# Expert 0's token weights read later, and the head's casts and patterns split between engines: a sorted-attention and expert-mixture kernel

## The chip, the cores and the metric

One core of a Trainium2 chip. TensorE (PE) multiplies matrices; VectorE (DVE), ScalarE (ACT) and GpSimd (POOL) do elementwise work; SyncE (SP) issues DMA transfers, as POOL does too. The metric is the device time of one execution in microseconds (us). The time before is the median of three runs, 358.14 us (358.12 to 358.28).

## The reference

Two stages, with 4 batches, 8 heads, 768 tokens a batch, head size 64, 8 blocks of 96 tokens, 4 experts, model width 512 and hidden width 1024.

```
P = sort_net                                  # 4 x 8 x 8 x 8
for _ in range(5):
    P = exp(P - max); P = P / row sums; P = P / column sums
k_sorted = einsum('bhij,bhjcd->bhicd', P, k blocks)     # and v_sorted
attn = softmax(scale * q_block @ k_sorted_block^T)
x = (attn @ v_sorted), as 3072 tokens x 512
p = domain_probs / (domain_probs.sum(-1) + 1e-9)        # 3072 x 4
out = sum over e of p[:, e] * (relu(x @ w1[e]) @ w2[e])
```

## The kernel before

The order of every engine's instructions is the order of the program's text (`tc.manual_schedule()`); the framework adds the waits that the data and the buffers need. There are two parts. The head (up to about 37 us) works on batch 0's attention and on the first layers; after it, the attention of the later batches is threaded between the experts' products.

The head goes like this. `sort_net` is loaded as `sn` (32 rows of one head and batch each, L77). Five rounds of exponential (ACT, L310), row sums and column sums (DVE, L315 to L321) follow; the last column scaling is done together with a spreading over 16 columns into `sn16` (L330), rows 0 to 3 by DVE and rows 4 to 7 by POOL. `r_half(a)` (L340) turns four rows of it round with four matmuls into PSUM tile `ps_R`. `build_PI0` (L352) multiplies that with the mask `maskk` into the pattern `PI0`, four heads at a time. `mix_half` (L511) multiplies natural keys or values by the pattern, for 4 heads (`qd`), after some warm-up matmuls (`keep_warm`, L504); `mixed` (L529) casts the result from PSUM into `kT` or `vT0`, for blocks `i0` to `i0+n` of four. `h_w` transposes mixed values (L548) and copies them out (L553); `h_s` makes scores (L576) and their exponential (L582); `h_a` multiplies by the values (L593) and normalizes (L606, L607); `h_x` transposes into `xT` with the permutation `perm` (L624, L628); `group0` runs expert 0's first layer (L704), `second_layer0` its second (L741).

Loads of q, k, v and weights are issued by POOL, in text order, and POOL waits before an issue when the eighth load before it hasn't landed. SP issues `sort_net`, the token probabilities `p_in` (L170) and `p_own` (L171: for the first 768 tokens, 128 partitions x 6 x 4 values). From `p_in`, `spread_weights` makes the normalized weights `p_out`, in steps between the rounds; its last step (L252) is followed by SP's store of the first rows (L256), the broadcast load `pb` (L230), which waits for that store, and the store of the rest (L258). From `p_own`, `own_weights` (L261) makes `p_sb`, expert 0's weight of a token, with four DVE instructions; `second_layer0` scales by it (L748). In the text `own_weights` stands after the second `group0(0, 1, 1, ...)` (L1435). DVE's later order is: casts of `h_k` and `h_v` (L532), the query copy (L301, of `h_q_both`, the second half on ACT), the copy L553, the scaling L748.

POOL's constants, `perm` (L200), the zeroed tails of `kT` and `ET` (L206, L210) and the ones in `vs0` (L215), stand before its part of `sn16`.

Of the kernel before, what the change touches and what calls it, by code (L numbers as in the profile page):

```python
# [11 lines left out]
F16 = mybir.dt.float16  # L12
# [6 lines left out]
def kernel(  # L19
# [11 lines left out]
    nc = tc.nc  # L31

    B, H, S, D = q.shape
    GH = B * H
    NB = sort_net.shape[-1]
    BLK = S // NB
# [3 lines left out]
    P = 128  # L40
    SCALE = float(D) ** -0.5

    CP = P // NB
    R = BLK // CP
# [3 lines left out]
    HB = NB // 2  # L48
    VW = D + 2
# [6 lines left out]
    const = ctx.enter_context(tc.tile_pool(name="const", bufs=1))  # L56
# [19 lines left out]
    sn = const.tile([GH, NB, NB], F32, name="sn")  # L76
# [10 lines left out]
    def from_spare(n):  # L87
        at = spare["at"]
        spare["at"] += n
        return Sflat[:, ds(at, n)]  # L90
# [37 lines left out]
    def head(b, nm, h):  # L128
        return natural[(b, nm, h // 4)][:, h % 4, :, :]
# [20 lines left out]
    def load_half_queries(hf):  # L150
        for qd in range(2):
            nc.gpsimd.dma_start(
                q0[ds(64 * qd, 64), hf].rearrange("p h r d -> p h (r d)"), half_queries(qd, hf)
            )
# [7 lines left out]
    def p_part(at, n):  # L162
        return Tt[2].rearrange("p a f x -> p (a f x)")[:, ds(2 * at, 2 * n)].bitcast(F32)
# [4 lines left out]
    p_own = p_part(2 * E * NT + NT, R * E).rearrange("p (t e) -> p t e", e=E)  # L168
    own_den = p_part(2 * E * NT + NT + R * E, R).rearrange("p (t o) -> p t o", o=1)
    nc.sync.dma_start(p_in, moe_domain_probs.rearrange("(p t) e -> p t e", t=NT))  # L170
    nc.sync.dma_start(p_own, moe_domain_probs[0:S].rearrange("(t p) e -> p t e", p=P))  # L171
    load_half_queries(0)
    load_natural(0, "k", 0)

# [1 line left out]
    ident = const.tile([P, P], F16, name="ident")  # L176
# [4 lines left out]
    for kc in range(0, NKC, 2):  # L181
# [15 lines left out]
    )  # L197

    perm = const.tile([BLK, BLK], F16, name="perm")
    nc.gpsimd.tensor_copy(  # L200
        perm.rearrange("p (c r) -> p c r", r=R), ident[0:BLK, 0:BLK].rearrange("p (r c) -> p c r", c=CP)
    )
    kTs, ETs, vs0s, wide = [], [], [], []
    for n in range(2):
        kT = const.tile([P, S + 32], F16, name=f"kT_{n}")
        nc.gpsimd.memset(kT[:, ds(S, 32)], 0.0)  # L206
        kTs.append(kT)
    for n in range(4):
        ET = const.tile([P, S + 32], F16, name=f"ET_{n}")
        nc.gpsimd.memset(ET[0:BLK, ds(S, 32)], 0.0)  # L210
        ETs.append(ET[0:BLK])
        wide.append(ET)
    for n in range(2):
        vs0 = from_spare(HB * 4 * VW)[0:BLK].rearrange("c (i s h w) -> c i s h w", i=HB, s=2, h=2)
        nc.gpsimd.memset(vs0[:, :, :, :, ds(D, 2)], 1.0)  # L215
        vs0s.append(vs0)
    vo = arena[:, ds(4 * NW + NQ + 4 * 4 * P, R * 4 * VW)].rearrange("p (r h w) -> p r h w", r=R, h=4)


# [6 lines left out]
    def load_p(b, c, es=range(E), pb=None):  # L226
        if pb is None:
            pb = moe.tile([P, E, 2 * P], F32, name=f"pb_{b}_{c}", tag="pb", bufs=1)
        n = len(es)
        nc.sync.dma_start(  # L230
            pb[:, ds(es[0], n)],
            p_dram[ds(es[0], n), ds(b * S + 2 * c * P, 2 * P)].rearrange("(o e) x -> o e x", o=1).broadcast_to(
                [P, n, 2 * P]
            ),
        )
        return pb
# [7 lines left out]
    def spread_weights():  # L244

        nc.vector.tensor_reduce(p_den, p_in, AX.X, ALU.add)
        yield
        nc.vector.tensor_scalar(out=p_den, in0=p_den, scalar1=1e-9, scalar2=None, op0=ALU.add)
        yield
        nc.vector.reciprocal(p_den, p_den)  # L250
        yield
        nc.vector.tensor_tensor(  # L252
            p_out.rearrange("p e t -> p t e"), p_in, p_den.broadcast_to([P, NT, E]), ALU.mult
        )
        p_rows = p_dram.rearrange("e (p t) -> p e t", t=NT)
        nc.sync.dma_start(p_rows[0:S_P], p_out[0:S_P])  # L256
        pbs[(0, 0)] = load_p(0, 0)
        nc.sync.dma_start(p_rows[S_P:P], p_out[S_P:P])  # L258
        yield

    def own_weights():  # L261

        nc.vector.tensor_reduce(own_den, p_own, AX.X, ALU.add)
        nc.vector.tensor_scalar(out=own_den, in0=own_den, scalar1=1e-9, scalar2=None, op0=ALU.add)
        nc.vector.reciprocal(own_den, own_den)
        nc.vector.tensor_tensor(p_sb[:], p_own[:, :, 0:1], own_den, ALU.mult)
# [38 lines left out]
    scol = const.tile([GH, NB, 1], F32, name="scol")  # L305
    sn16 = const.tile([GH, NB, NB, CP], F16, name="sn16")
# [19 lines left out]
            if it:  # L326
                next(p_steps)

    for a, eng in enumerate((nc.vector, nc.gpsimd)):
        eng.tensor_tensor(  # L330
            sn16[:, ds(a * HB, HB)],
            sn[:, ds(a * HB, HB)].rearrange("g i (j o) -> g i j o", o=1).broadcast_to([GH, HB, NB, CP]),
            scol[:].rearrange("g j (i o) -> g i j o", i=1).broadcast_to([GH, HB, NB, CP]),
            ALU.mult,
        )

    ps_R = psM.tile([P, 2, 512], F32, tag="ps", name="ps_R")
    Rv = ps_R[:, :, 0:HB * GH].rearrange("p a (i g) -> p a i g", g=GH)
# [11 lines left out]
    Rs = const.tile([P, GH, NB], F16, name="Rs")  # L350

    def build_PI0(eng, a, h0, hn, src):  # L352
        eng.tensor_tensor(
            PI0[a][:, ds(h0, hn)],
            maskk[:, 0:HB * CP].rearrange("p (o i c) -> p o i c", o=1, c=CP).broadcast_to([P, hn, HB, CP]),
            src.rearrange("p g (i o) -> p g i o", o=1).broadcast_to([P, hn, HB, CP]),
            ALU.mult,
        )
# [18 lines left out]
            )  # L377

    r_half(0)
    for h0 in range(0, H, 4):  # L380
        build_PI0(nc.vector, 0, h0, 4, Rv[:, 0, :, ds(h0, 4)].rearrange("p i g -> p g i"))
    vec, act = nc.vector.tensor_copy, nc.scalar.copy


# [126 lines left out]
    def mix_half(nm, qd, hf, pool, warm_up=0):  # L511

        ps = pool([P, 1024], F32, f"ps_m{nm}_{qd}_{hf}")
        keep_warm(ps[:, 0:P], warm_up)
        tails[(nm, qd, hf)] = ps[:, 2 * R * 64:1024].bitcast(F16).rearrange("p (n x) -> p n x", n=2)
        ps = ps[:, 0:2 * R * 64].rearrange("p (s r x) -> p s r x", s=2, r=R)
        for sg in range(2):
            for r in range(R):
                for hh in range(2):
                    h = 4 * qd + 2 * sg + hh  # L520
                    nc.tensor.matmul(  # L521
                        ps[ds(D * hh, D), sg, r, :],
                        head(0, nm, h)[:, r, :],
                        PI0[hf][:, h, :, :].rearrange("p i c -> p (i c)"),
                        start=True, stop=True,
                    )
        return ps

    def mixed(nm, qd, ps, i0, n, copy):  # L529

        dst = kTs[qd][:, 0:S] if nm == "k" else vT0[qd]
        copy(  # L532
            dst.rearrange("p (i x c) -> p x i c", i=HB, c=CP)[:, :, ds(i0, n)],
            ps.rearrange("p s r (i c) -> p (s r) i c", c=CP)[:, :, ds(i0, n)],
        )
# [4 lines left out]
    def h_v(qd, hf, copy, pool=psa):  # L540
        mixed("v", qd, mix_half("v", qd, hf, pool), 0, HB, copy)
# [24 lines left out]
    def h_s(qd, qq, ps=None):  # L566

        kT, ET = kTs[qd], ETs[2 * qd + qq % 2]
        if ps is None:
            ps = psa([P, 2, 512], F32, f"ps_s0_{qd}_{qq}")  # L570
        for n in range(4):
            for hh in range(2):
                sg, i = n // 2, 2 * (qq % 2) + n % 2

                m = BLK if 2 * i + sg == 3 else P
                nc.tensor.matmul(  # L576
                    ps[0:m, hh, ds(n * BLK, BLK)],
                    kT[ds(D * hh, D), ds((2 * i + sg) * BLK, m)],
                    qT0[qd][ds(D * hh, D), sg, qq // 2, :, ds((2 * (qq % 2) + n % 2) * CP, CP)],
                    start=True, stop=True,  # L580
                )
        nc.scalar.activation(  # L582
            ET[:, 0:S].rearrange("c (h x) -> c h x", h=2), ps[0:BLK, :, 0:HS],
            AF.Exp, bias=0.0, scale=SCALE,
        )
# [426 lines left out]
    for e in range(E):  # L1012
        w, hk, hf = w1sb[e], NKC // 2, FF // 2
# [380 lines left out]
    ]  # L1394


    mk0 = mix_half("k", 0, 0, psm, 8)
    mixed("k", 0, mk0, 0, 2, act)
    mv0 = mix_half("v", 0, 0, psa)
    mixed("v", 0, mv0, 0, 2, vec)  # L1400
    r_half(1)
    act(Rs.rearrange("p g (a i) -> p a g i", a=2), Rv.rearrange("p a i g -> p a g i"))
    h_s(0, 0)
    mixed("k", 0, mk0, 2, 2, act)
    load_half_queries(1)
    load_w2(0, 2)
    build_PI0(nc.gpsimd, 1, 0, H, Rs[:, 0:H, HB:NB])
# [24 lines left out]
    even01()  # L1432
    w11(vec)
    group0(0, 1, 1, [0, 1])
    own_weights()  # L1435
    ps_s11 = ps_a10
    h_s(1, 1, ps_s11)
    evacuate00 = group0(0, 1, 0, [2, 3], True)
# [9 lines left out]
    group0(1, 1, 0, [2, 3])  # L1448
    h_v(0, 1, vec)
    h_v(1, 1, vec)  # L1450
    group0(1, 1, 1, [2, 3])


# [66 lines left out]
    for g in range(G0 + 1):  # L1520
        b, c = divmod(g, R // 2)
# [56 lines left out]
```

## Time and profile before

| | |
|---|---|
| median of 3 runs | 358.14 us |
| the profiled execution | 358.21 us |
| its span, first to last instruction | 356.3 us |
| PE busy | 350.4 us (98% of the span) |
| DVE, ACT, POOL busy | 277.5, 170.1, 137.6 us |
| DMA packets, software queue (POOL's issues) | 38720, 19.93 MB |
| DMA packets, hardware queue (SP's issues) | 35856, 19.67 MB |
| store L256: issue, length of the issue, issue to landing | 19.99 us, 0.35 us, 5.5 us |
| load L171: issue, issue to landing | 1.66 us, 3.9 us |

The span is what the profile covers; 1.9 us of the execution lie around it. A line of the profile names the engine, the source line, the operation, what is written and read, and, in square brackets, how long the engine sat idle before it and what ended that. PEld is TensorE's weight load, which overlaps its matmuls. Instructions are issued in order on each engine, so a wait holds up all that is behind it on that engine.

### The profile page before, as it was taken

The numbers are of one execution on the slowest core, as the hardware profiler recorded it, in microseconds if no ns is written. First come the engines' busy times: TensorE is split into PE (matmuls) and PEld (weight loads), VectorE is DVE, ScalarE is ACT, GpSimd is POOL, SyncE is SP. The second block draws the span as 40 slices with busy tenths as digits, with TensorE's granted clock in tenths as the row PEclk, the third lists the DMA queues.
The fourth block names the chain that finished last, engine by engine and source line by source line (L and its number), as shares of the span: only waits on it lengthen the run. The fifth ranks groups of instructions, "written<-read, shape, count | busy, mean of one in ns | idle before, by whom it ended". The sixth has DMA issues, their size and how long they took to land.

```text
span 356.3 us, 9511 instructions
## 1 busy us (share of the span) xinstructions
PE 350.4 (98%) x3948; PEld 305.5 (86%) x3948; DVE 277.5 (78%) x555; ACT 170.1 (48%) x302; POOL 137.6 (39%) x154
## 2 busy tenths in 40 slices
PE   8899999999999999999999999999999999999996
PEld 8686857888888888988899888888888888888886
DVE  5766787779798687778879988896678886588963
ACT  2653330452425445368847259830288611598301
POOL 8766112466022420000626318840068800188400
PEclk9999999999999999999999999999999999999999
DMA  8999999999999999743995410005200014100021
GB/s 104 203 205 230 212 209 194 207 195 167 195 180 166 195 116 203 138 88 44 180 205 91 107 74 0 2 1 136 78 26 3 2 37 141 62 0 2 0 75 46
DMA packets 74762, 40.26 MB, mean 113 GB/s; under 512 B 41568, under 2 KB 70496, under 8 KB 74720
## 3 DMA queue, kind: packets, MB, share of 16 engines
q0 software_dynamic: 38720, 19.93, 43.2%
q1 hardware_dynamic: 35856, 19.67, 27.2%
q8 instruction: 31, 0.51, 0.6%
q14 instruction: 11, 0.09, 0.1%
q10 hardware_dynamic: 144, 0.07, 0.1%
HBM read 41.88 MB, written 6.34 MB: 135 GB/s over the span
## 4 chain that ended last, share of the span: by engine, by line
PE 95%; DVE 3%; issue 0%; DMA 0%; ACT 0%; DVEq 0%
PE ps_h L815 18%; PE ps_Q L1296 18%; PE ps_p L799 12%; PE ps_X L1153 10%; PE ps_Z L1153 7%; PE ps_Q L1153 7%; PE ps_Z L1296 6%; PE ps_h L704 3%; PE ps_o L741 3%; PE ps_p L860 3%; PE ps_a L479 2%; PE ps_s L444 2%; PE ps_k L425 1%; PE ps_v L391 1%; PE ps_mv L521 1%; PE ps_a L593 0%
## 5 line engine op out<-in xcount | busy, mean ns | idle before, releaser
L815 PE MATMUL ps_h<-xT,w 128*128 128x256 f16 x576 | 67.5, 273 | 0.0
L815 PEld LDWEIGHTS <-w 128*128 128x128 f16 x576 | 55.2, 98 | 7.3
L821 DVE SCALAR_TENSOR_TENSOR Hb<-ps_h,pb 128x1024 f16<-128x1024 f32 x34 | 41.5, 1223 | 17.8 <-PE ps_h L815 17.6
L1153 PEld LDWEIGHTS <-w 128*128 128x128 f16 x480 | 43.6, 98 | 4.7
L1166 POOL TENSOR_TENSOR arena<-tmp,pb 128x512 f16<-128x512 f32 x12 | 15.2, 1276 | 65.7 <-PE ps_Z L1153 49.8
L1296 PEld LDWEIGHTS <-Hb 128*128 128x128 f16 x320 | 31.1, 98 | 3.5
L1165 ACT ACTIVATE tmp<-tmp 128x512 f32<-128x512 f32 x46 | 29.0, 632 | 3.9 <-DVE tmp L1203 3.9
L1296 PEld LDWEIGHTS <-Sb 128*128 128x128 f16 x304 | 28.2, 98 | 3.0
L1153 PEld LDWEIGHTS <-arena 128*128 128x128 f16 x312 | 27.7, 98 | 2.8
L451 ACT ACTIVATE ET<-ps_s 96x768 f16<-96x768 f32 x24 | 18.1, 802 | 25.2 <-PE ps_s L444 25.0
L434 ACT CAST kT<-ps_k 64x384 f16<-64x384 f32 x48 | 22.7, 473 | 13.3 <-PE ps_k L425 12.3
L126 POOL DMA_DIRECT2D arena<-in_q_dram x24 | 19.9, 842 | 20.8 <-DMA q_ring<-arena 17.7
L1153 PE MATMUL ps_X<-ET,arena 128*128 128x256 f16 x168 | 25.2, 272 | 0.0
L1296 PE MATMUL ps_Q<-w,Hb 128*128 128x256 f16 x192 | 24.6, 273 | 0.0
L799 PEld LDWEIGHTS <-Hb 128*128 128x128 f16 x232 | 21.9, 98 | 3.0
L1159 DVE SCALAR_TENSOR_TENSOR Hb<-ps_X,pb 128x512 f16<-128x512 f32 x27 | 18.7, 692 | 7.0 <-PE ps_X L1153 7.0
L1173 ACT COPY ps_X<-ps_Z 128x512 f32<-128x512 f32 x27 | 15.4, 571 | 17.8 <-PE ps_Z L1153 17.8
L1153 PE MATMUL ps_Z<-xT,w 128*128 128x256 f16 (+1 forms) x176 | 22.5, 258 | 0.0
L785 DVE TENSOR_TENSOR Sb<-Hb 128x512 f16<-128x512 f16 x33 | 20.6, 646 | 0.0
L1180 ACT COPY tmp<-ps_X 128x512 f32<-128x512 f32 x26 | 15.2, 586 | 9.2 <-PE ps_X L1153 6.6
L1159 DVE SCALAR_TENSOR_TENSOR Hb<-ps_Z,pb 128x512 f16<-128x512 f32 x27 | 18.4, 683 | 1.3 <-PE ps_Z L1153 1.3
L1203 DVE TENSOR_TENSOR tmp<-ps_Q,tmp 128x512 f32<-128x512 f32 x26 | 17.7, 683 | 0.8 <-PE ps_Q L1153 0.8
(270 smaller groups left out, 744.3 us busy)
## 6 DMA issues: line engine op xcount, KB each, us to landing
w<-in_moe_w_dram POOLq DMA_DIRECT2D x4, 1024.0 KB, 27.2
w<-in_moe_w_dram POOLq DMA_DIRECT2D x6, 512.0 KB, 19.7
arena<-in_k_dram POOLq DMA_DIRECT2D x7, 384.0 KB, 7.6
arena<-in_v_dram POOLq DMA_DIRECT2D x7, 384.0 KB, 8.1
vs<-arena SPq DMA_DIRECT2D x36, 66.0 KB, 5.3
arena<-in_q_dram POOLq DMA_DIRECT2D x24, 96.0 KB, 7.5
out_dram<-ob SPq DMA_DIRECT2D x9, 256.0 KB, 2.0
pb<-p_dram SPq DMA_DIRECT2D x4, 512.0 KB, 5.8
```

Of the source, the lines that this page charges most:

```text
L126: nc.gpsimd.dma_start(t[:, h // 2, :, h % 2, :], q[b, h].rearrange("(t p) d -> p t d", p=P))
L434: nc.scalar.copy(kT[ds(D * hh, D), r], pk[ds(D * r, D), hh].rearrange("p a (i c) -> p a i c", c=CP),)
L451: nc.scalar.activation(ETs[2 * (pr % 2) + hh][:, 0:S].rearrange("c (a x) -> c a x", a=2), pss[hh][0:BLK, :, 0:HS], AF.Exp, bias=0.0, scale ...
L785: tt(sm[0], blk(0, 1), blk(1, 1), ALU.add)
L799: nc.tensor.matmul(ps, lhs(e, f), Ts[e][rhs][:, f, :], start=(first and e == es[0] and f == 0), stop=(done and e == es[-1] and f == KH - 1 ...
L815: nc.tensor.matmul(ps[:, f, :], w1sb[e][:, kc, ds((4 * g + f) * P, P)], xT[:, kc, ds(2 * c * P, 2 * P)], start=(kc == 0), stop=(kc == NKC ...
L821: nc.vector.scalar_tensor_tensor(out=Hb[:, homes.get(e, e), ds(4 * g, 4), :], in0=ps[:], scalar=0.0, op0=ALU.max, in1=weights(e).broadcast ...
L1153: nc.tensor.matmul(dst[:, ds(f * cols, cols)], a[lhs][:, k, ds((f0 + f) * P, P)], t[rhs][:, k, :], start=(first and f == 0 and k == 0), st ...
L1159: nc.vector.scalar_tensor_tensor(out=home(i, j), in0=src.rearrange("p (f x) -> p f x", f=m), scalar=0.0, op0=ALU.max, in1=weight(j).broadc ...
L1165: nc.scalar.activation(src, src, AF.Relu, bias=0.0, scale=1.0)
L1203: tt(t12, Q, u2, ALU.add)
L1296: nc.tensor.matmul(ps, lhs(e, f), Ts[e][rhs][:, f, part], start=(first and e == 0 and f == 0), stop=(e == E - 1 and f == KH - 1), skip_gro ...
```

## The change

- SP's load of `p_own` moves from third place, at the start, to behind the store of the first normalized rows.
- `own_weights` moves from after `group0(0, 1, 1, [0, 1])` to after `h_v(1, 1, vec)`.
- The constants move from ahead of POOL's part of `sn16` to behind it, `perm` last of them; the zeroing of `ET` covers 128 rows for 96.
- `sn16`: DVE makes rows 0 to 2 (384 elements a row for 512), POOL row 3 and then rows 4 to 7.
- `PI0`'s first half is built in parts of 2, 2 and 4 heads for 4 and 4.
- The first `mix_half` has 4 warm-up matmuls for 8.
- The first casts: of blocks 0 and 1 of the keys ACT takes one and DVE the other, and likewise of the values; blocks 2 and 3 of the keys are two ACT instructions for one.
- `h_s(0, 0)` stands ahead of `r_half(1)`, and the copy `Rs` is DVE's for ACT's.

```
     nc.sync.dma_start(p_in, moe_domain_probs.rearrange("(p t) e -> p t e", t=NT))
-    nc.sync.dma_start(p_own, moe_domain_probs[0:S].rearrange("(t p) e -> p t e", p=P))
...
-    nc.gpsimd.tensor_copy(
-        perm.rearrange("p (c r) -> p c r", r=R), ident[0:BLK, 0:BLK].rearrange("p (r c) -> p c r", c=CP)
-    )
...
-        nc.gpsimd.memset(kT[:, ds(S, 32)], 0.0)
...
-        nc.gpsimd.memset(ET[0:BLK, ds(S, 32)], 0.0)
...
-        nc.gpsimd.memset(vs0[:, :, :, :, ds(D, 2)], 1.0)
...
+    def fill_constants():
+        for kT in kTs:
+            nc.gpsimd.memset(kT[:, ds(S, 32)], 0.0)
+        for ET in ETs:
+            nc.gpsimd.memset(ET[:, ds(S, 32)], 0.0)
+        for vs0 in vs0s:
+            nc.gpsimd.memset(vs0[:, :, :, :, ds(D, 2)], 1.0)
+        nc.gpsimd.tensor_copy(
+            perm.rearrange("p (c r) -> p c r", r=R), ident[0:BLK, 0:BLK].rearrange("p (r c) -> p c r", c=CP)
+        )
...
         nc.sync.dma_start(p_rows[0:S_P], p_out[0:S_P])
+        nc.sync.dma_start(p_own, moe_domain_probs[0:S].rearrange("(t p) e -> p t e", p=P))
         pbs[(0, 0)] = load_p(0, 0)
...
-    for a, eng in enumerate((nc.vector, nc.gpsimd)):
+    for eng, i0, n in ((nc.vector, 0, HB - 1), (nc.gpsimd, HB - 1, 1), (nc.gpsimd, HB, HB)):
         eng.tensor_tensor(
-            sn16[:, ds(a * HB, HB)],
+            sn16[:, ds(i0, n)],
...
+    fill_constants()
...
-    for h0 in range(0, H, 4):
-        build_PI0(nc.vector, 0, h0, 4, Rv[:, 0, :, ds(h0, 4)].rearrange("p i g -> p g i"))
+    for h0, n in ((0, 2), (2, 2), (4, 4)):
+        build_PI0(nc.vector, 0, h0, n, Rv[:, 0, :, ds(h0, n)].rearrange("p i g -> p g i"))
...
-    mk0 = mix_half("k", 0, 0, psm, 8)
-    mixed("k", 0, mk0, 0, 2, act)
+    mk0 = mix_half("k", 0, 0, psm, 4)
+    mixed("k", 0, mk0, 0, 1, act)
+    mixed("k", 0, mk0, 1, 1, vec)
     mv0 = mix_half("v", 0, 0, psa)
-    mixed("v", 0, mv0, 0, 2, vec)
+    mixed("v", 0, mv0, 0, 1, vec)
+    mixed("v", 0, mv0, 1, 1, act)
+    h_s(0, 0)
     r_half(1)
-    act(Rs.rearrange("p g (a i) -> p a g i", a=2), Rv.rearrange("p a i g -> p a g i"))
-    h_s(0, 0)
-    mixed("k", 0, mk0, 2, 2, act)
+    vec(Rs.rearrange("p g (a i) -> p a g i", a=2), Rv.rearrange("p a i g -> p a g i"))
+    for i in (2, 3):
+        mixed("k", 0, mk0, i, 1, act)
...
     group0(0, 1, 1, [0, 1])
-    own_weights()
...
     h_v(0, 1, vec)
     h_v(1, 1, vec)
+    own_weights()
     group0(1, 1, 1, [2, 3])
```

More of the change, by code (lines that the diff above doesn't have):

```diff
@@ L199 @@
     perm = const.tile([BLK, BLK], F16, name="perm")
-    nc.gpsimd.tensor_copy(
-        perm.rearrange("p (c r) -> p c r", r=R), ident[0:BLK, 0:BLK].rearrange("p (r c) -> p c r", c=CP)
-    )
     kTs, ETs, vs0s, wide = [], [], [], []
     for n in range(2):
-        kT = const.tile([P, S + 32], F16, name=f"kT_{n}")
-        nc.gpsimd.memset(kT[:, ds(S, 32)], 0.0)
-        kTs.append(kT)
+        kTs.append(const.tile([P, S + 32], F16, name=f"kT_{n}"))
     for n in range(4):
         ET = const.tile([P, S + 32], F16, name=f"ET_{n}")
-        nc.gpsimd.memset(ET[0:BLK, ds(S, 32)], 0.0)
         ETs.append(ET[0:BLK])
@@ L213 @@
     for n in range(2):
-        vs0 = from_spare(HB * 4 * VW)[0:BLK].rearrange("c (i s h w) -> c i s h w", i=HB, s=2, h=2)
-        nc.gpsimd.memset(vs0[:, :, :, :, ds(D, 2)], 1.0)
-        vs0s.append(vs0)
+        vs0s.append(from_spare(HB * 4 * VW)[0:BLK].rearrange("c (i s h w) -> c i s h w", i=HB, s=2, h=2))
+    def fill_constants():
[8 more added lines that the diff above has]
+        )
     vo = arena[:, ds(4 * NW + NQ + 4 * 4 * P, R * 4 * VW)].rearrange("p (r h w) -> p r h w", r=R, h=4)
@@ L327 @@
                 next(p_steps)
-    for a, eng in enumerate((nc.vector, nc.gpsimd)):
+    for eng, i0, n in ((nc.vector, 0, HB - 1), (nc.gpsimd, HB - 1, 1), (nc.gpsimd, HB, HB)):
         eng.tensor_tensor(
-            sn16[:, ds(a * HB, HB)],
-            sn[:, ds(a * HB, HB)].rearrange("g i (j o) -> g i j o", o=1).broadcast_to([GH, HB, NB, CP]),
-            scol[:].rearrange("g j (i o) -> g i j o", i=1).broadcast_to([GH, HB, NB, CP]),
+            sn16[:, ds(i0, n)],
+            sn[:, ds(i0, n)].rearrange("g i (j o) -> g i j o", o=1).broadcast_to([GH, n, NB, CP]),
+            scol[:].rearrange("g j (i o) -> g i j o", i=1).broadcast_to([GH, n, NB, CP]),
             ALU.mult,
         )
+    fill_constants()
     ps_R = psM.tile([P, 2, 512], F32, tag="ps", name="ps_R")
```

## The prediction

> **What bounds the kernel now.** I read the busy time by stage first, then the chain of waits through the first 45 us, then the engines' timeline around the two places that the edit touches, and last the DMA packets by queue.
>
> The busy time by stage (columns: stretch, length, then busy time of PE, PEld, DVE, ACT, POOL, granted clock, DMA share, GB/s):
>
> ```profile
> 10.40:20.00 9.60, 7.80 (x197) 6.70 (x198) 6.62 (x17) 5.68 (x10) 7.33 (x18) 1.00 1.28 204
> 28.70:36.90 8.20, 8.09 (x134) 4.79 (x134) 5.43 (x10) 2.61 (x5) 4.02 (x5) 1.00 1.20 231
> 36.90:356.00 319.10, 316.50 (x3278) 277.73 (x3278) 252.92 (x486) 152.99 (x274) 111.04 (x104) 1.00 0.66 105
> ```
>
> From 36.9 us on TensorE is busy 316.5 of 319.1 us. What the first 37 us lose or gain arrives at the end nearly whole. Between 10.4 and 20 us TensorE has 1.8 us of holes, and the chain shows who makes them:
>
> ```profile
> 11.60 0.26 PE ps_R L342 x4
> 11.86 0.55 PE ps_mk L507 x8
> 12.45 0.57 PE ps_mk L521 x24
> 13.01 0.39 PE ps_mv L521 x24
> ...
> 13.43 0.57 DVE Sb L532
> ...
> 14.04 0.44 PE ps_mv L548 x4
> ...
> 14.57 0.42 DVE Sb L553
> ```
>
> The head's chain runs: sort matrix (L342), warm-up (L507), mixing products of keys and values (L521), the cast of the mixed values by DVE (L532), its transposes (L548), DVE's copy (L553). The reader should keep 14.04, the start of the first transposes. The second place is 15 us later; here is the timeline of DVE, ACT and PE:
>
> ```profile
> 27.70 0.95 DVE L532 CAST Sb<-ps_mv 128x768 f16<-128x768 f32 x1
> ...
> 29.61 0.56 DVE L301 COPY Sb<-ps_q 128x768 f16<-128x768 f16 x1 [0.96 <-PE ps_q L288]
> ...
> 30.18 0.69 DVE L553 COPY Sb<-ps_w 96x1024 f16<-96x1024 f16 x1
> 30.20 0.80 ACT L301 COPY Sb<-ps_q 128x768 f16<-128x768 f16 x1 [1.43 <-DVE Sb L301]
> 30.93 0.24 PEld L576 LDWEIGHTS <-kT 64*128 64x128 f16 x10 [0.42 <-issue]
> ```
>
> DVE's copies L301 and L553 end at 30.87, and the score matmuls L576, which wait for that L553, start at 30.94. So DVE is already the last one in at this point: whatever delays L301 delays TensorE one for one. Before L301 DVE is idle 0.96 us, and that hole is all the room there is.
>
> **The change, part by part: the head.** The sort matrix: DVE's cast shrinks from 512 to 384 elements a row. L330 took 0.68 us for 512, and L321 took 0.21 for 64, so 1.05 ns an element: 0.55, a gain of 0.13. Row 3 goes to POOL (128 elements), bounded by POOL's L193 of 16 elements (0.22) and its L330 of 512 (1.23): by the line between them 0.45. POOL's constants are out of its way, so it starts when the column sums are ready (10.83) and ends near 11.35, before the fourth matmul needs it (some 11.6). The constants (0.18+0.31+0.19+0.35 busy, run together between 10.44 and 11.25) now follow both POOL pieces, which end near 12.5. They are done by 13.4, well before the first reader at about 14.6. The two query loads behind them on POOL slide from 12.40 to 13.4; they landed at 22 to 23 behind a full queue and are read at 28.7: nothing.
>
> So the four matmuls start at 11.46 for 11.60. Four warm-ups instead of eight (69 ns each) end near 12.0. The first pattern piece is 128 elements; L353 takes 0.42 for 256 and DVE's L532 takes 0.56 for 384, so 0.28: it runs 11.83 to 12.11, and the products start at 12.16 for 12.45. The second piece is ready just as the first twelve products have issued. Keys are mixed by 12.75 (13.02 before), values by 13.13 (13.39). That is a gain of 0.27.
>
> Then the casts. In the changed order each second part carries a wait for the other engine's first part: DVE's key piece waits for ACT's key piece, ACT's value piece for DVE's value piece. They are dealt to two engines, but run in turn. ACT takes 0.48 for 384 elements and 0.82 for 768, so 0.31 for 192; DVE 0.56 and 0.96, so 0.36; consecutive DVE instructions overlap by 0.07. ACT's key piece 12.78 to 13.09, DVE's key piece 13.12 to 13.48, DVE's value piece 13.41 to 13.77, ACT's value piece 13.80 to 14.11. The transposes wait for both value pieces: 14.16, where they stood at 14.04. The gain of 0.27 turns into a loss of 0.12. The exponential on ACT slips from 13.97 to 14.05 and ends before its reader. The `Rs` copy, now DVE's, ends near 14.46, ahead of L553 at 14.69; POOL's pattern for the second half reads it at 17.16. Bounds: if the pairs ran side by side the transposes would start at 13.56, 0.48 earlier, but the last value load landed at 16.10 and its products began at 16.15, so no more than 0.06 would be left; above, POOL's piece as long as its 1.23 row adds 0.6. I take +0.12.
>
> [...]
>
> **The change, part by part: expert 0's weights.** `own_weights` (four DVE instructions, 21.13 to 21.92: 0.80) leaves a stretch where DVE then idled 1.10: no gain. It now stands behind the last value cast, in front of L301, and its first instruction waits for its load. That load was issued by SP at 1.66 and landed in 3.9 us, needed at 21; at 1.66 it cost the other loads nothing, as the two views of packets below show. Now SP issues it right behind the store L256 (19.99 to 20.34), so at about 20.4 to 20.9. Packets by queue, for 3.8 to 4.4 us (when this load last ran), 29 to 33 us and 24.2 to 29.2 us:
>
> ```profile
> q0 software_dynamic: 151, 0.12, 123.4%
> q1 hardware_dynamic: 151, 0.00, 33.9%
> ```
>
> ```profile
> q0 software_dynamic: 323, 0.59, 79.5%
> q1 hardware_dynamic: 319, 0.33, 29.6%
> ```
>
> ```profile
> q0 software_dynamic: 794, 1.03, 117.4%
> q1 hardware_dynamic: 40, 0.01, 2.2%
> ```
>
> q0 carries POOL's loads, q1 SP's. While both have work they go one for one, 151 to 151 and 323 to 319, whatever the sizes. q0 is full from 4 us to past 60. The load has 128x6 pieces of 16 bytes, 768 packets, so it needs 768 of q0's. The store issued by 20.34 landed 5.5 us after its issue, at 25.5, with most of its 128 packets done by 24.2, and the next entry on q1 goes on from there. In the 5.0 us from 24.2 q0 moved 794 packets; 768 take 4.85, so 29.05. The store's landing came 0.4 after its packets on most engines: 29.45. The head's +0.12 reaches the store's issue too, and 35.0 to 36.0, where 96-byte packets rode along, shows q0 at 183 a us for some 205 alone, which for 768 packets is up to 0.5. I take a landing at 29.8, between 29.0 (packets from 23.9, no slowing) and 31.0 (172 ns for each of the big packets of the last part plus 15 for ours).
>
> DVE is free at 28.65+0.12. It waits until 29.8, spends 0.80+0.03, and L301 starts at 30.63 for 29.61: 1.0 late. Behind it stand L553 and the scaling L748; ACT's L301 waits for DVE's, TensorE's L576 for L553: 31.95 for 30.94. The head's 0.12 is swallowed in this wait. Next on SP the weight broadcast L230 (25.51) goes behind the 768 packets, begins some 0.4 later than its 29.03 and lands near 36.4; it is read at 38.79 plus the delay: nothing. Nothing later gives time back, TensorE being full.
>
> **Sum:** +1.0 us on the profiled execution's 358.21 is 359.2; the median of 358.14 lies 0.07 below that execution, which I leave inside the rounding.
>
> **The rivals.** (a) The weights land in time: one mechanism, at DVE's own_weights. If q1's 16-byte packets pass several to one of q0's, the load lands before 28.8 and own_weights fits the 0.96 hole. For it: the first load took 3.9 us from issue. Against: it was 151 to 151 whenever q0 was full. Only the head's +0.12 remains: 358.3, no change. From a landing of 29.5 on it decides past 0.2%. (b) The load is slower still: the later q0 packets are 2 KB, and each pair costs more; landing 31.0, +2.2: 360.4. For it the pairs of 29 to 33 us, 213 ns with 1 KB on q1; against, 16 bytes are little to move. (c) The head does gain, the parts side by side and the early loads sooner without the 768 packets: 151 of those took 34% of the engines' 0.6 us, by that rate 1.0 us for all 768, enough to let the casts' 0.48 through; head -0.5, and weights in time: 357.7. For it the 0.27 gained up to the casts; against, the two waits and q0's 151 packets in 0.6 us, its usual rate. [...]
>
> **How the numbers follow.** My forecast 0.60, (a) 0.20, (b) 0.13, (c) 0.07. Predicted 359.2. The range runs from 358.1, which takes in most of (a), to 360.3, most of (b). 0.2% is 0.72 us, about what a measurement here can tell from no change. Slower by more than that: (b) and 0.55 of the forecast's 0.60, together 0.68; within: (a), the forecast's other 0.05 and 0.02 of (c), together 0.27; faster: the part of (c) whose gain goes beyond its sum, 0.05.
>
> **What would show it.** Right: in the changed profile DVE idles about 1 us before own_weights' reduction, released by a DMA of `T`, near 29.8; ACT's L301 and PE's score matmuls follow late; q1 has 768 packets of 16 bytes between 24 and 29.5. The first transposes start at 14.1 to 14.3, and DVE's key piece starts after ACT's ends. Wrong: own_weights done by 29.6, or transposes before 13.9.

## The result: slower, and by five times the forecast

Eight executions of the changed kernel have a median of 363.26 us (361.26 to 368.83), eight of the kernel before, taken beside them, 358.21 (357.81 to 358.90). The ratio is 1.0131, 95% interval 1.0113 to 1.0149: some 4.7 us lost, where 1.0 was forecast and 360.3 was the end of the range. The ratios here and below leave out executions that took over 1.5% longer than the kernel's fastest; of these eight that is the two above 368 us.

The changed kernel's profiled execution took 368.83 us; a late load near 198 us, far from the change, adds a wait of 3.3 us to it, so only the first 40 us or so of its trace are compared. The lines have moved: L301, L532, L553, L576 and L748 of before are L305, L537, L558, L581 and L753 now.

The busy time by stage (columns as in the prediction), the last stretch to the end of this longer span:

```profile
10.40:20.00 9.60, 7.67 (x177) 6.40 (x178) 6.06 (x17) 5.64 (x12) 7.73 (x19) 0.82 1.25 197
28.70:36.90 8.20, 4.96 (x90) 3.25 (x88) 3.73 (x9) 2.37 (x4) 3.88 (x5) 0.89 1.22 225
36.90:366.00 329.10, 323.98 (x3334) 281.91 (x3332) 254.57 (x492) 153.97 (x276) 111.03 (x104) 0.99 0.66 102
```

Between 28.7 and 36.9 us TensorE is busy 4.96 us; it was 8.09. So the loss sits at the second place of the prediction. There is also something new in the column of the granted clock: 0.82 and 0.89, where both stretches had 1.00.

Who makes the hole is in the chain of waits (start, length, engine and line):

```profile
21.48 0.30 SPq L259
21.78 0.04 issue
21.82 11.84 DMA T<-in_moe_domain_probs_dram
...
33.68 0.19 DVE T L267
...
34.33 0.17 DVE p_sb L270
34.49 0.06 DVE Sb L305
34.55 0.32 issue
34.88 0.69 DVE Sb L558
35.56 0.04 issue
35.60 0.82 PE ps_s L581 x16
```

It is the chain that was forecast, link by link: SP's load of `p_own`, the four steps of `own_weights` (L267 to L270), the query copy L305, the copy L558, the scores L581. The reader should compare the numbers with it: the load goes out at 21.82 (20.4 to 20.9 was forecast), lands 11.84 us later (9 or so), and the scores start at 35.60 where they stood at 30.94. The timeline shows the two waits at the ends of it:

```profile
33.68 0.18 DVE L267 TENSOR_REDUCE T<-T 128x6 f32<-128x24 f32 x1 [3.68 <-DMA T<-in_moe_domain_probs_dram]
...
35.60 0.82 PE L581 MATMUL ps_s<-Sb,kT 64*128 64x96 f16 x16 [3.24 <-DVE Sb L558]
```

And the head, in the chain of waits:

```profile
11.08 0.56 DVE sn L334
...
11.68 0.23 PE ps_R L347 x3
11.91 0.03 issue
11.94 0.20 PE ps_R L347
...
12.58 0.59 PE ps_mk L526 x24
...
13.19 0.33 ACT kT L537
13.52 0.02 issue
13.54 0.36 DVE kT L537
13.90 0.27 DVE Sb L537
14.17 0.02 issue
14.19 0.33 ACT Sb L537
14.52 0.04 issue
14.56 0.50 PE ps_mv L553 x4
```

Three sort matrix matmuls run at 11.68; the fourth, for POOL's row, at 11.94. Then the four cast parts run strictly one behind the other, as forecast. This execution does its sort rounds 0.22 later than the profiled one of before (last column scaling at 11.08 for 10.86; most profiles below have 11.08), so starts are best counted from that step: the transposes come 3.48 after it, and came 3.18 after it before.

### The profile page after: what moved, and what is told of

The parts are those of the page before. It is cut to its first block, busy times and chain, and to the rows that moved or that the text cites. A ratio compares the mean times of both kernels' runs of the same rounds, so it can differ in the third digit from the quotient of the medians.

```text
span 366.8 us, 9508 instructions
## 1 busy us (share of the span) xinstructions
PE 354.2 (97%) x3944; PEld 307.9 (84%) x3944; DVE 275.8 (75%) x558; ACT 170.0 (46%) x303; POOL 138.1 (38%) x155
## 4 chain that ended last, share of the span: by engine, by line
PE 88%; DMA 6%; DVE 3%; ACT 1%; issue 1%; SPq 0%; DVEq 0%; ACTq 0%
PE ps_Q L1301 17%; PE ps_h L820 17%; PE ps_p L804 12%; PE ps_X L1158 9%; PE ps_Z L1301 6%; PE ps_Q L1158 6%; PE ps_Z L1158 6%; DMA T<-in_moe_domain_probs_dram 3%; DMA w<-arena 3%; PE ps_o L746 3%; PE ps_p L865 3%; PE ps_a L484 2%; PE ps_s L449 2%; PE ps_h L709 1%; PE ps_k L430 1%; PE ps_v L396 1%
## 5 line engine op out<-in xcount | busy, mean ns | idle before, releaser
L1301 PE MATMUL ps_Q<-w,Hb 128*128 128x256 f16 x192 | 25.7, 281 | 0.0
L790 DVE TENSOR_TENSOR Sb<-Hb 128x512 f16<-128x512 f16 x33 | 18.7, 589 | 1.2 <-POOL Hb L1171 1.2
```

The costliest lines, as they stand in the source:

```text
L790: tt(sm[0], blk(0, 1), blk(1, 1), ALU.add)
L1301: nc.tensor.matmul(ps, lhs(e, f), Ts[e][rhs][:, f, part], start=(first and e == 0 and f == 0), stop=(e == E - 1 and f == KH - 1), skip_gro ...
```

## The experiments

All kernels ran against the kernel before on the same chips. Starts are counted from the last column scaling on VectorE (L330 before, L334 after) of the same profiled execution; "landing" is that of the `p_own` load, from the start of the span.

| kernel | landing | first transposes | scores L581 | span | median us | ratio to before, 95% interval |
|---|---|---|---|---|---|---|
| before | in time | +3.18 | +20.08 | 356.3 | 358.14 | |
| changed | 33.7 | +3.48 | +24.52 | 366.8 | 363.26 | 1.0131 (1.0113 to 1.0149) |
| weights alone | 32.0 | +3.18 | +22.84 | 360.6 | 362.55 | 1.0122 (1.0095 to 1.0150) |
| head alone | in time | +3.48 | +20.77 | 357.0 | 359.23 | 1.0033 (1.0017 to 1.0049) |
| load early | in time | +3.49 | +21.86 | 358.0 | 360.13 | 1.0055 (1.0036 to 1.0073) |
| 128 packets | 27.1 | +3.49 | +21.91 | 358.1 | 360.11 | 1.0062 (1.0035 to 1.0090) |
| stall kept warm | 32.3 | +3.74 | +23.20 | 360.0 | 363.91 | 1.0140 (1.0111 to 1.0170) |
| head, 8 warm-ups | in time | +3.52 | +20.83 | 363.3 | 359.54 | 1.0026 (1.0015 to 1.0036) |
| head, casts whole | in time | +3.20 | +20.34 | 356.9 | 358.94 | 1.0021 (1.0000 to 1.0043) |
| load early, sums in PSUM | in time | +3.48 | +22.05 | 358.1 | 360.03 | 1.0049 (1.0031 to 1.0067) |
| load early, at the reader | in time | +3.49 | +20.38 | 356.9 | 358.55 | 1.0015 (1.0000 to 1.0029) |
| load late, at the reader | 31.7 | +3.50 | +20.38 | 356.2 | 359.41 | 1.0026 (1.0012 to 1.0039) |
| head, sort whole | in time | +3.56 | +20.65 | 358.6 | 359.54 | 1.0033 (1.0014 to 1.0051) |
| three repairs | in time | +3.12 | +20.01 | 356.1 | 358.44 | 1.0007 (0.9995 to 1.0020) |

### Which part costs: the weights or the head

The weights' part alone, on the kernel before:

```
-    nc.sync.dma_start(p_own, ...)              # behind p_in's load
     nc.sync.dma_start(p_rows[0:S_P], p_out[0:S_P])
+    nc.sync.dma_start(p_own, ...)
...
-own_weights()                                  # after group0(0, 1, 1, [0, 1])
...
 h_v(1, 1, vec)
+own_weights()
```

> The kernel before with the weights' part alone: the load of p_own behind the store of the normalized weights and own_weights at its new place; the head's sort matrices, fills and casts are those of before. Theory (the wait of own_weights for its late load is the main loss): the store issues as it did before, near 20.0 us, so the load lands earlier than in the changed kernel (33.7): about 30.0 to 31.5, the score matmuls start 32.2 to 33.5 instead of 30.9, and the time is 359.4 to 360.7; if TensorE's granted clock drops after the stall, another 1.3 us (DVE's shift over that stretch in the changed kernel), 360.7 to 362. Rival (the head's dealing of casts, pieces and fewer warm-ups is the loss): about 358.2, as before.

The head's part alone, the changed kernel with those lines undone:

> The changed kernel with the weights' part undone: the load of p_own at the start, own_weights at its old place. Theory (weights' wait is the main loss): 358.2 to 359.2; the fourth R matmul 0.26 late and the casts one behind the other make the first transposes some 0.3 later, and a half clock window of 3.4 us after the head's gaps would add up to 0.7. Rival (the head is the loss): 361 or more, near the changed kernel's 363.3.

Measured: 362.55 for the weights alone, 359.23 for the head alone. The weights are the main loss: they alone cost 1.0122 of the changed kernel's 1.0131. The head came out at the upper end of its expected price, the weights beyond theirs. The chain of waits of the weights' part alone:

```profile
20.25 0.30 SPq L255
20.56 0.04 issue
20.60 11.39 DMA T<-in_moe_domain_probs_dram
...
33.93 0.58 PE ps_s L576 x16
```

Here the head is that of before, and the load goes out at 20.60, just where the prediction had it. It still lands at 31.99, 2.2 us after the forecast 29.8. So it is the duration that was mis-sized. The packets by queue in 24.2 to 27 us and in 27 to 30.2 us of that run (columns: packets, MB, share of 16 engines):

```profile
q0 software_dynamic: 519, 0.56, 117.1%
q1 hardware_dynamic: 516, 0.01, 25.8%
```

```profile
q0 software_dynamic: 340, 0.64, 107.0%
q1 hardware_dynamic: 340, 0.02, 17.4%
```

One for one holds, 519 to 516 and 340 to 340. The pace is q0's, and q0's falls from 185 packets a us to 106 as its packets grow from 1.1 KB to 1.9 KB (0.56 MB by 519, 0.64 by 340). But this fall was in the forecast: its stretch of the kernel before, 24.2 to 29.2 us, has it too (546 of q0's packets in 24.2 to 27, 322 in 27 to 30.2). In the same stretch this run has:

```profile
q0 software_dynamic: 766, 1.01, 113.8%
q1 hardware_dynamic: 763, 0.02, 21.6%
```

That is 766 for the forecast's 794, 4% fewer. The size and start of each single packet in the trace show what was left out. The load's first packet starts at 24.43. Of q1's 763 packets only 677 are the load's; 68 of the others are 96-byte packets of the store, which was not done yet. The load's last 91 packets then take from 29.2 to 31.57, and they are only 91 of the 210 that q1 moves up to 31.6: 106 are already 1 KB packets of the next transfer on q1. So the load doesn't end everywhere together. Most of it is through by the time that the mean pace gives, and the landing waits for stragglers. Why these lag isn't shown. In the changed kernel the load takes 11.84 us from its issue, for 11.39 here.

### Is it the packets, or the place behind the store

The same place, but six rows in a run for each partition: 128 packets of 96 bytes.

```
-nc.sync.dma_start(p_own, moe_domain_probs[0:S].rearrange("(t p) e -> p t e", p=P))
+nc.sync.dma_start(p_own, moe_domain_probs[0:S].rearrange("(p t) e -> p t e", t=R))
```

> The changed kernel with p_own read as six rows in a run for each partition, 128 packets of 96 bytes in place of 768 of 16, from the same place behind the store; expert 0's weights then go to other tokens, so the output is another. Theory (it is the count of small packets, each of which takes its turn with one of the other queue, 768 of them in about 7 us at 100 pairs per us): the load lands near 26 to 28 us, own_weights waits for nothing, and the time is that of the load put back to the start, 358.2 to 359.5. Rival (the place behind the store and the next loads sets it, whatever the packets): it lands after 31 and the time stays above 361.

And the load put back to the start, `own_weights` left at its new place:

> The changed kernel with the load alone put back to the start; own_weights stays at its new place on VectorE's queue. Theory (the wait for the load costs, not where own_weights stands): the same as the head alone within 0.3 us, with VectorE's L305 not waiting for any DMA and the score matmuls some 3 us earlier than at 35.6. Rival (two VectorE and ScalarE steps right ahead of the scores' queries cost by their place): 0.8 to 1 us above the head alone, since L305's two steps stand between the third values' cast and the queries' copy.

Measured: the load of 128 packets, issued at 21.71, lands at 27.14; it takes 5.4 us in place of 11.8. So the count of packets makes the landing. In the time the two kernels agree (360.11 and 360.13): once the load is in time it doesn't matter how. But both are 0.9 above the head alone, and their scores 1.1 later. The theory had excluded this; the rival, the place on VectorE's queue, had forecast it. The timeline of the early load shows what the place costs:

```profile
29.31 1.04 POOL L377 TENSOR_TENSOR arena<-maskv,Rs 128x512 f16<-128x512 f16 x1
...
29.99 0.17 DVE L267 TENSOR_REDUCE T<-T 128x6 f32<-128x24 f32 x1
...
30.19 1.20 DVE L268 TENSOR_SCALAR T<-T 128x6 f32<-128x6 f32 x1
30.32 1.04 POOL L369 TENSOR_TENSOR arena<-maskk,Rs 128x512 f16<-128x512 f16 x1
...
31.43 0.19 DVE L269 RECIPROCAL T<-T 128x6 f32<-128x6 f32 x1
31.65 0.17 DVE L270 TENSOR_TENSOR p_sb<-T 128x6 f32<-128x6 f32 x1
31.73 0.55 DVE L305 COPY Sb<-ps_q 128x768 f16<-128x768 f16 x1
```

No load is waited for. Yet L268, which adds a constant to six numbers a partition and took 0.17 us before (L264), takes 1.20 and ends at 31.39, when POOL's last pattern product ends (30.32 + 1.04 = 31.36). With 128 packets it is the same: L268 runs from 30.10 to 31.45, POOL's product from 30.39 to 31.43. The prediction had measured the hole, 0.96, against the steps' 0.80 at their old place, where POOL made no products.

### Is it POOL's hold on that step

The row sums go to a bank of PSUM that nothing else uses then; the steps and their place stay:

```
-def own_weights():
+def own_weights(own_den):
...
     po = psm([P, 2, 512], F32, f"ps_o_{col}")
+    if col == 0:
+        own_weights(po[:, 1, 0:R].rearrange("p (t o) -> p t o", o=1))
```

> The changed kernel with the load at the start (360.1), and the row sums of own_weights kept in a PSUM bank that holds nothing then, in place of SBUF; the same four steps at the same place. There the step that adds 1e-9 (L268) took 1.20 us where the same step takes 0.17 elsewhere, and ended with POOL's product of the pattern matrices (30.32 + 1.04 = 31.36). [...] Rival (place on the queue, 0.8 us of work in a hole too short for it): no gain, 360.1.

The timeline:

```profile
29.13 1.04 POOL L377 TENSOR_TENSOR arena<-maskv,Rs 128x512 f16<-128x512 f16 x1
29.29 0.17 DVE L268 TENSOR_SCALAR ps_o<-ps_o 128x6 f32<-128x6 f32 x1
29.50 0.20 DVE L269 RECIPROCAL ps_o<-ps_o 128x6 f32<-128x6 f32 x1
29.74 0.16 DVE L270 TENSOR_TENSOR p_sb<-T,ps_o 128x6 f32<-128x6 f32 x1
...
29.95 1.04 PE L748 MATMUL ps_o<-w,Hb 128*128 128x512 f16 x4 [1.51 <-DVE p_sb L270]
...
31.81 0.56 DVE L305 COPY Sb<-ps_q 128x768 f16<-128x768 f16 x1 [1.92 <-PE ps_q L292]
```

With its operands in PSUM the step isn't held: L268 runs inside one of POOL's products (29.13 to 30.17) and takes 0.17, where it took 1.20 with them in SBUF. The 1.03 gained there doesn't reach the time, 360.03 for 360.13, and the last two lines show where it went: the sums lie in the tile that L748 fills, so TensorE now waits 1.51 us for L270, and L305 waits for TensorE. One wait took the other's place.

### Is it the wait, or what stands behind it

`own_weights` moved behind the query copies, directly ahead of its first reader, with the load early and with the load late:

```
-h_v(1, 1, vec)
-own_weights()
+h_v(1, 1, vec)
...
+            if col == 0:
+                own_weights()
             oaccs[col] = room[:, col - 2] if col > 1 else moeo.tile(...)
```

> The changed kernel with the load at the start (360.1) and the four steps of own_weights moved on VectorE's queue from ahead of the query copies to behind them, directly ahead of the first L753 that reads p_sb. There POOL's pattern products are over or nearly so, and what waits behind the steps is an eviction and not the scores' queries. Theory (in the changed kernel's place the 1e-9 step is held until POOL's products end, and the query copies behind it with it): L305 follows PE's query transposes as in the head alone, the score matmuls start near 31.9, L268 takes under 0.5 us, and the time is 359.2 to 359.5. Rival (0.8 us of VectorE work costs about the same at either place): 360.1.

> The same place of own_weights, with the load behind the store as in the changed kernel, so that it still lands at 32 to 33.7. Theory (it is the place of the wait on VectorE's queue, ahead of the query copies, that turns the late load into 3 us): the score matmuls start near 31.9 as in the head alone, only the first eviction of second layer outputs and what follows it on VectorE's queue are late, by 1 us or less, and the time is 359.5 to 360.5. Rival (whatever waits for the load on VectorE, the next step behind it is late by as much and the end with it): 361.5 or more.

Measured: 358.55 with the load early and 359.41 (358.24 to 359.85) with it late; both below what was expected. The timeline with the late load:

```profile
30.47 0.69 DVE L558 COPY Sb<-ps_w 96x1024 f16<-96x1024 f16 x1
...
31.23 0.52 PE L581 MATMUL ps_s<-Sb,kT 64*128 64x96 f16 x16
...
31.73 0.18 DVE L267 TENSOR_REDUCE T<-T 128x6 f32<-128x24 f32 x1 [0.56 <-DMA T<-in_moe_domain_probs_dram]
...
32.64 0.75 DVE L755 TENSOR_SCALAR oacc<-ps_o,p_sb 128x512 f32<-128x512 f32 x1
```

The load lands at 31.70, which counted from the last column scaling is as late as in the weights' part alone (20.85 for 20.90), and the scores run at 31.23 all the same. What is late now is L755, the scaling of expert 0's outputs as they are copied out of PSUM, and TensorE has other work meanwhile. So of the changed kernel's 4.7 us the wait as such cost little; that the query copies stood behind it cost nearly all, together with what the clock did behind that stall (below): eight of the nine executions here kept the full clock. With the load early, L268 took 0.57 us, against an expected 0.5 at most. POOL was then issuing a load (31.23 to 32.10), and L268 ended at 32.07. The early load gives one number more: its scores come 0.39 earlier than those of the head alone, which differs in nothing but `own_weights` at its old place. In the head alone VectorE's reciprocal L611 started 0.51 after the matmuls it waits for, and 0.11 after them without `own_weights` ahead of it. Why isn't shown.

### The head's parts

The first casts whole again, keys by ScalarE and values by VectorE:

```
-mixed("k", 0, mk0, 0, 1, act)
-mixed("k", 0, mk0, 1, 1, vec)
+mixed("k", 0, mk0, 0, 2, act)
 mv0 = mix_half("v", 0, 0, psa)
-mixed("v", 0, mv0, 0, 1, vec)
-mixed("v", 0, mv0, 1, 1, act)
+mixed("v", 0, mv0, 0, 2, vec)
```

> The head alone (359.2), with the first casts whole again as in the kernel before: the first two key columns one ScalarE cast, the first two value columns one VectorE cast. Theory (the four halves run one behind the other, 13.2 to 14.5, and delay the transposes): the first transposes come 0.3 earlier against the sort matrices' last step, and the time is 358.5 to 358.9. Rival (the sort matrices' piece that waits for POOL's product is the head's loss): no gain, 359.1 to 359.3.

The last column scaling in two halves and the first patterns in two steps again, the casts dealt:

```
-for eng, i0, n in ((nc.vector, 0, HB - 1), (nc.gpsimd, HB - 1, 1), (nc.gpsimd, HB, HB)):
+for eng, i0, n in ((nc.vector, 0, HB), (nc.gpsimd, HB, HB)):
...
-for h0, n in ((0, 2), (2, 2), (4, 4)):
+for h0, n in ((0, 4), (4, 4)):
```

> The head alone (359.2) with the sort matrices' last product in two halves on the two engines and the first patterns in two steps, as in the kernel before; the casts stay dealt in parts. Theory (the piece on POOL brings its matmul 0.26 us late and takes back what the shorter VectorE piece gains): 358.9 to 359.2, a gain of 0 to 0.3. Rival (the dealt pieces help): 359.3 to 359.6.

Measured: whole casts bring the transposes from +3.48 to +3.20, so the casts, one behind the other, make nearly all of the head's delay there. The time, 358.94, is 0.3 below the head alone's, which the intervals can't tell apart. Whole sort matrices bring the transposes to +3.56: the dealt pieces gain 0.08, which is the rival's outcome; the time, 359.54, can't be told from the head alone either. The timeline of the whole sort matrices shows something else:

```profile
11.08 0.68 DVE L334 TENSOR_TENSOR sn<-sn,scol 32x512 f16<-32x512 f32 x1
11.12 1.54 POOL L334 TENSOR_TENSOR sn<-sn,scol 32x512 f16<-32x512 f32 x1 [0.71 <-DVE scol L323]
```

POOL's half, started beside VectorE's, takes 1.54 us and ends 0.90 after it. In the kernel before it took 1.23, having started later (11.23 for 10.86), and also ended 0.92 after VectorE's. In the changed kernel POOL's row of 128 elements took 0.76 and ended 0.25 after VectorE's piece; a quarter of 0.90 is 0.23. So in all three POOL's end is what it would be if POOL did its work only once VectorE was done; what holds POOL back isn't shown.

### The clock

In the changed kernel's profile TensorE's clock is granted at half for 3.41 us from 14.69 and again from 35.17 (and from 202.42, behind the load near 198); the weights' part alone has such a window from 34.63; the profile of before has none. The profiles of the early load and of the 128 packets have the first window too, that of the head alone doesn't. The eight executions of the changed kernel fall in order by their mean clock: 361.26 us at 1.0, 362.65 and 362.75 at 0.995, 363.23 to 364.38 at about 0.99, and the two above 368 at 0.99 and 0.985. The weights' part alone doesn't keep this order: 361.47 and 364.38 at 1.0, 362.24 to 363.15 at 0.995. Two kernels were to say what the windows are worth. One fills the stall with 45 matmuls of a constant:

```
+            if col == 0:
+                keep_warm(po[:, 1, 0:P], 45)
             oaccs[col] = room[:, col - 2] if col > 1 else moeo.tile(...)
```

> The changed kernel with 45 matmuls of a constant added on TensorE ahead of the stalled scores, into a PSUM bank that holds nothing then, so that TensorE is not idle while VectorE waits for the load. Theory (the stall's own 3 us is joined by a halved TensorE clock right behind it, since TensorE had idled 3.24 us): no window of share 0.5 after 33 us, and 0.6 to 1.3 us below the changed kernel, near 361.5 to 362.5. Rival (the clock behind the stall costs nothing, other engines set the pace there): the time of the changed kernel, 363.3, whatever the clock does.

The other gives the head alone its eight warm-ups back (`mix_half("k", 0, 0, psm, 8)`):

> The head alone (weights' part undone, 359.2), with the 8 warm-up matmuls of the kernel before in place of 4 ahead of the first mixing. If the four fewer are what drops the clock in the head in some executions: the clock stays 1.0 in all, and the time is 358.9 to 359.1 with less spread. If the head's other idle stretches set it: the same clock windows and time as the head alone, 359.2.

Measured: with the stall filled, no window of half clock is left before the end of the profiled execution, but three of the five executions have a mean clock of 0.986 to 0.991; the median is 363.91 (361.99 to 368.94), no gain. From the scores to the end the profiled executions do differ: the weights' part, with its half clock, is 4.1 later than before at the end and 2.76 at the scores, so 1.35 more; with the stall filled, 3.56 and 3.12, so 0.44 more. That puts the half clock at some 0.9 us, from one execution each, but over the executions it doesn't show: filled, one at full clock took 361.99 and another at full clock 363.91. With eight warm-ups the mean clock was 0.999 or above in 12 of 13 executions, for 8 of 11 of the head alone; the time was 359.54, no better than the head alone (359.23). So in the time it is the rival's outcome for both; whether eight warm-ups keep the clock up more often, so few executions don't decide. How much of the changed kernel's loss is clock stays open.

### The three repairs together

Load at the start, `own_weights` at its reader, whole casts; the dealt sort matrices, the late fills and the order of the first scores stay.

> The changed kernel with the load at the start, own_weights directly ahead of its first reader, and the first casts whole again; the sort matrices' pieces, the later fills and the order of the first scores stay as changed. If the three costs found (the late load, the place ahead of the query copies, the casts one behind the other) add, this is the 358.55 of the early load with own_weights at its reader less some 0.3 for the casts: 358.1 to 358.4, no different from the kernel before. If the freed 0.9 us of VectorE at 21 to 22 us is worth something to the head, 357.7 to 358.0, faster than both. If the casts' gain is lost in a wait behind them: 358.5.

Measured: 358.44, ratio 1.0007 (0.9995 to 1.0020). This lies between the first expectation and the last, which the spread can't tell apart. With the three costs taken out no loss is left that can be measured, and no gain: transposes 0.06 and scores 0.07 earlier than before. No version here beats the kernel before.

## Why the prediction was right about the place and wrong about the size

- **The chain: right.** Slower, through DVE's wait for the load at `own_weights`, with L305, L558 and the scores behind it. The late-load kernel with `own_weights` at its reader shows that this order is the cause, since with the same late load its scores come at +20.38, as they do with the load early.
- **The landing: the term that failed.** The step was "In the 5.0 us from 24.2 q0 moved 794 packets; 768 take 4.85, so 29.05", and from it 29.8. With the issue as forecast the load landed at 31.99. The turns one for one held, and so did the pace, 766 packets in that stretch. But the count took every packet of q1 from 24.2 on as the load's, where 86 weren't, and it took the mean over all of the queue for the end: by 29.05 some 660 of the 768 were through, the last one started at 31.55, and the landing came 0.4 after that, as forecast. Rival (b), with larger packets and 31.0, was nearer and also short. At the scores this makes +2.76 for the forecast 1.0; the profiled execution loses another 1.35 from there to the end, where it has its half-clock window.
- **The issue: right where the clock is full.** 20.4 to 20.9 was forecast, with the head's 0.12 in it. The weights alone have 20.60, and the late load at the reader, whose sort rounds are as early as before's, 20.67. The 21.82 of the changed kernel stands behind its first half-clock window (14.69 to 18.10). Counted from the last column scaling the load goes out at +10.74 there and at +10.63 with 128 packets, which has that window too; at +10.11 with the stall kept warm and +9.82 with the late load at the reader, which have none; and at +9.51 in the weights alone. So in the runs without the window the head delays the issue by 0.3 and 0.6, about what it delays their transposes (0.32 and 0.56), where 0.12 had been put; where the window stands the issue is another 0.5 to 0.9 later. The landing moves with it: 33.7 in the changed kernel, 32.3 with the stall kept warm.
- **The price of being in time: wrong.** Rival (a) put `own_weights` into the 0.96 hole at its old 0.80 and came to 358.3. With the load in time it took 1.83, from L267 at 29.99 to p_sb at 31.82, and the kernel 360.1.
- **The head: right in kind, short in size.** The casts in turn, with +0.12 at the transposes; measured +0.30. The missing part is POOL's row: 0.45 was forecast, to 11.35, "before the fourth matmul needs it"; it took 0.76, and its matmul came 0.26 behind the other three. It ended 0.25 after VectorE's piece, about a quarter of the 0.92 and 0.90 by which POOL's halves ended after VectorE's in the kernel before and with whole sort matrices; what held it isn't shown. The head alone cost 0.9 at the end: at the scores `own_weights` at its old place had added 0.39, which was put at nothing.
- **Not thought of: the clock**, as told above; its share is open.

## What to carry to other kernels

Before a wait is moved, ask what stands behind it on its engine; a load landing near 32 us cost 4.4 us ahead of the query copies (1.0122) and under 1 us behind them (1.0026, the head's parts included). A transfer of many tiny pieces that takes turns with another queue is priced to its last packet, not at the mean pace: here a tenth of the packets took the last 2 us of 7. A stretch where an engine idles is a hole only for instructions that its neighbour's work in that stretch doesn't hold up: here L268 took 1.20 us beside POOL's products, 0.17 at the old place in the kernel before.

## What the hardware did that was not expected

A six-element VectorE step from SBUF to SBUF was held for 1.0 us by POOL's products, and not just by the one that was running: asked for at 30.19, while a product ran to 30.35, it ended only when the next had ended too. The sum ahead of it (L267, a reduction, 0.17) was not held. In the head alone the same step took 0.31 and ended at 22.02, 0.04 after a copy of POOL's (21.68 to 21.98). With its operands in PSUM the step took 0.17 inside one of POOL's products (29.13 to 30.17), and from SBUF to SBUF it took 0.17 in the changed kernel at 33.90, where POOL idled. Why one is held and the other not isn't shown.

TensorE's clock fell to half for 3.41 us after stretches that were not idle throughout. In the weights' part alone TensorE was idle 2.70 us in one piece and busy 0.71 of the 3.41 us before the drop (31.22 to 34.63); in the changed kernel's head it was busy 2.54 of the 3.41 before (11.28 to 14.69), and the head alone, busy 2.53 of the same 3.41, kept its full clock in the execution profiled. What dropped the clock in the head isn't shown.
